# Block 0's feed-forward in two times 256 rows, gate and up with rows as stationary side, and query products at full rate: an adaLN transformer block on one Trainium2 core

## The chip, the cores and the metric

The kernel runs on one core of a Trainium2 chip. The metric is the device time of one execution in microseconds (us). The core's engines are TensorE (PE; its weight loads are shown as PEld), VectorE (DVE), ScalarE (ACT), GpSimd (POOL) and the queue of SyncE (SP), which issues the transfers here. Each engine works through its own instructions in order and waits on semaphores that the others raise.

## The reference

Inputs: 2048 rows of 512, all float32. Computed is one block with layer norms that a condition `c` scales and shifts:

```
mod = silu(c) @ w_mod                      # six rows of 512: sa, ca, ga, sb, cb, gb
h   = layernorm(x) * (1 + ca) + sa
q   = (h @ wq) in 32 heads of 16;  k = h @ wk;  v = h @ wv      # one k and v for all heads
p   = softmax(q @ k.T * 16**-0.5)
x   = x + ga * ((p @ v) @ wo)
h   = layernorm(x) * (1 + cb) + sb
x   = x + gb * ((sigmoid(h @ w_gate) * (h @ w_up)) @ w_down)    # 512 -> 1792 -> 512
```

## The kernel before

**Attention is the main line.** 2048 queries are cut into 8 query blocks of 256, the 32 heads into 4 groups of 8. A *unit* is one query block with one group, so there are 32 units (`units`), and each unit walks over the 16 blocks of 128 keys: 512 *steps*, each in two half-steps. In a step PE makes four score tiles `st` (128 keys by 512), whose exponentials ACT writes to `P`; four score tiles `sa` for a later unit (its row maxima are needed beforehand), which DVE reduces to `mx`; and, two steps late (`LAG`), the products of `P` and the values into `craw`. These are made in tiles of the array of 64 by 32, eight at a time (`columns`). At the end of a unit ACT copies `craw` to `cs`, and `place`, `recip` and `finish` normalise it with a round trip through DRAM; the last step of POOL gives `a`, the input of the output projection.

**Side work goes in between.** At the end of each half-step `piece` may append some products that don't belong to attention. A *term* is one product of 128 by 128 by 512 in float16 (every operand is split in a high and a low half and each product takes three passes); as side work a term is 8 matmuls of 64 by 32. Two groups of terms run together as a `Couple`, one in each half of the array's rows, and take both of the two PSUM banks that side work has. Side work is, in this order: the query products that the prologue left over (`q`, 5 couples of 24 terms), and for each block of 512 rows the output projection (`wo`, 2 couples of 24 terms), the norm on DVE and POOL, transposes (`tr`), gate and up (`gu`, 14 couples of 24 terms), and down (`dn`, 168 terms). Blocks 0, 1 and 2 are done inside the loop, and block 3 after it (the tail), with what is left of block 2 ahead of it.

**The planner.** `pick` chooses the next group, `plan` and `places` spread it over half-steps. The rates are terms for each half-step: `QRATE` 0.55 for query products up to step `FIRST`, `RATE` 2.2 for all else; `ERATE` applied only to early pieces, which `AHEAD` = 0, 0, 0, 0 switched off. Block `b` is handed over at query block 2b+1 (its first 256 rows: one `wo` couple and two `tr`) and at 2b+2 (everything else). A `wo` couple starts `SKIP` = 9 steps after its hand-over, a `tr` `GAP` = 2 steps after the norm is marked; if the next group isn't ready a spare one may go first, and if there is none, the half-step has no side work. `KEPT` = 2 groups at each block's end are kept as spares.

**Gate and up.** `gu_group(p, m)` holds the weights as the stationary side (128 of the 1792 columns) and moves `h2` (512 rows), so its result already stands with columns on partitions, as `dn` needs it. For each p ACT takes tanh of the gate's bank, DVE copies the up bank to `u`, and POOL makes (tanh + 1) * u and splits it in `gh` and `gl` (`gated`). `dn` comes in two parts (8 and 6 of the 14 pieces), each with its own read-out.

**Weights.** 46 jobs (`split_weight`) load the feed-forward's weights, scale and split them on POOL, and store gate's and up's to DRAM (`wD`), from where `ask` loads them back to the tiles `gw` (four of 512 KB, `GWB`), one for each p. 42 jobs are spread over the first `WSTEPS` = 110 steps. The last four overwrite the memory that holds the query weights (`wqh`, `wql` are parts of `wdh`, `wdl`), and come from step `WLAST` = 175 on.

## Time and profile before

| | us |
|---|---|
| median of 3 runs | 1707.36 (1706.1 to 1709.64) |
| profiled execution | 1703.12 |
| its span on the core | 1701.3 |
| prologue, to the first exponential of the loop | 105.6 |
| loop of 512 steps, to the end of the last `cs` copy | to 1559.9 |
| tail (block 2's rest and block 3) | 1559.9 to 1701.3 |

The engines overlap, so busy times don't add up; the question at any place is which of them the others wait for. The copy `cs` on ACT, once for each unit, is a good clock: from the end of one to the end of the next lie 16 steps. In what follows *unit n* in a time sense is the stretch that ends with the nth such copy, counted from 0; because of the lag of two steps it covers steps 16n+2 to 16n+17. A PE row of a group gives the time in which at least one of its matmuls ran, which overlaps with that of other groups.

### The profile page before, as it was taken

What the parts mean: (1) busy time and instruction counts of PE and PEld (TensorE: products, weight loads), DVE (VectorE), ACT (ScalarE), POOL (GpSimd) and SP (SyncE); (2) the same over time, 40 slices, a digit from 0 to 9 for tenths busy, and PEclk for the clock granted to TensorE, in tenths of its full rate; (3) what the DMA queues carried; (4) which work ended last, traced back from release to release, by engine and by line L of the source; (5) the groups of instructions that cost most, each with busy time, mean ns of one, the idle gap of its engine ahead of it and who ended that gap; (6) DMA issues with size and microseconds to landing.
All of it is one profiled execution on the core that took longest, in us unless ns stands there. A gap on an engine that the chain in (4) does not pass through costs nothing.

```text
span 1701.3 us, 88793 instructions
## 1 busy us (share of the span) xinstructions
PE 1657.1 (97%) x40226; PEld 997.2 (59%) x40226; DVE 1427.7 (84%) x2428; ACT 1287.3 (76%) x2335; POOL 610.2 (36%) x784
## 2 busy tenths in 40 slices
PE   6999999999999999999999999999999999999998
PEld 3335555555456666666656676666666676654443
DVE  7799999989999999999999999999999999912311
ACT  5558898878988888888888888888888888884100
POOL 4432554553242451232443232223442332132423
PEclk9989999999999999999999999999999999999999
DMA  7121333320121110111021110010121110011211
GB/s 243 54 62 49 107 104 99 110 77 21 29 62 50 58 54 14 40 28 28 28 77 52 50 42 13 28 37 25 38 77 41 52 53 16 23 47 52 87 50 38
DMA packets 86726, 94.12 MB, mean 55 GB/s; under 512 B 24916, under 2 KB 65868, under 8 KB 86348
## 3 DMA queue, kind: packets, MB, share of 16 engines
q1 hardware_dynamic: 86348, 88.44, 16.8%
q8 instruction: 315, 5.16, 1.3%
q14 instruction: 63, 0.52, 0.1%
HBM read 67.82 MB, written 16.24 MB: 49 GB/s over the span
## 4 chain that ended last, share of the span: by engine, by line
PE 81%; DVE 11%; ACT 3%; SPq 2%; DMA 2%; issue 1%; POOL 1%; POOLq 0%; ACTq 0%; DVEq 0%
PE craw L135 21%; PE pgu L135 15%; PE sa L135 13%; PE st L135 12%; DVE mx L135 8%; PE pd L135 7%; PE pgu L186 5%; PE pd L186 3%; PE po L135 2%; PE pq L135 2%; SPq L135 1%; ACT P L135 1%; DVE st L135 1%; DMA xall<-in_A_x_dram 1%; DMA lc<-lD 1%
## 5 line engine op out<-in xcount | busy, mean ns | idle before, releaser
L135 DVE TENSOR_REDUCE mx<-sa 128x1 f32<-128x512 f32 x2048 | 1288.6, 682 | 82.3 <-PE st L135 40.5
L135 ACT ACTIVATE P<-st 128x512 f32<-128x512 f32 x2048 | 1167.4, 597 | 226.2 <-PE st L135 168.6
L135 PE MATMUL craw<-P,V 64*32 64x512 f32 x8192 | 1094.7, 599 | 1.3 <-ACT cs L135 0.5
L135 PE MATMUL sa<-kp,qp 64*32 64x512 f16 (+1 forms) x7940 | 834.7, 379 | 13.1 <-DVE mx L135 12.4
L135 PE MATMUL st<-qp,kp 64*32 64x512 f16 x8192 | 837.6, 379 | 4.9 <-ACT P L135 4.2
L135 PEld LDWEIGHTS <-kp 64*32 64x32 f16 x8192 | 333.9, 91 | 215.9 <-issue 93.4
L135 PEld LDWEIGHTS <-qp 64*32 64x32 f16 (+1 forms) x7940 | 288.4, 92 | 149.6 <-issue 74.2
L135 PE MATMUL pgu<-h2h,gw 64*32 64x512 f16 x5248 | 285.4, 376 | 0.6
L135 PEld LDWEIGHTS <-gw 64*32 64x32 f16 x7872 | 181.7, 92 | 66.8 <-issue 25.1
L135 PEld LDWEIGHTS craw<-P,V 64*32 64x32 f32 x8192 | 184.0, 105 | 23.7 <-PE craw L135 4.1
L135 PE MATMUL pgu<-h2l,gw 64*32 64x512 f16 x2624 | 178.8, 376 | 1.2 <-issue 1.0
L135 PE MATMUL craw<-nought 64*32 64x1 f16 x1050 | 171.2, 163 | 0.0
L897 POOL TENSOR_SCALAR th<-th 128x512 f32<-128x512 f32 x41 | 25.4, 620 | 355.0 <-ACT th L135 298.2
L135 PEld LDWEIGHTS <-nought 64*32 64x32 f16 x1050 | 97.7, 93 | 71.9 <-issue 51.5
L556 POOL MEMSET qp<- 32x1024 f16 x60 | 56.7, 945 | 79.3 <-PE st L135 57.2
L320 POOL TENSOR_SCALAR wst<-wst 128x512 f32<-128x512 f32 x46 | 28.6, 621 | 155.5 <-DMA wst<-in_B_w_up_dram 103.2
L135 PE MATMUL pd<-wdl,gh 64*32 64x512 f16 x1152 | 79.2, 376 | 0.0
L135 PE MATMUL pd<-wdh,gh 64*32 64x512 f16 x1152 | 77.3, 376 | 0.1
L135 PE MATMUL pd<-wdh,gl 64*32 64x512 f16 x1152 | 76.6, 376 | 0.0
L186 PE MATMUL pgu<-h2h,gw 128*128 128x512 f16 x240 | 71.9, 379 | 1.5 <-DVE h2h L355 1.5
L891 ACT ACTIVATE th<-pgu 128x512 f32<-128x512 f32 x15 | 9.0, 597 | 82.1 <-PE pgu L186 82.1
L135 DVE COPY u<-pgu 128x512 f32<-128x512 f32 x41 | 28.0, 682 | 50.1 <-PE pgu L135 50.1
(160 smaller groups left out, 1436.9 us busy)
## 6 DMA issues: line engine op xcount, KB each, us to landing
gw<-wD SPq DMA_DIRECT2D x56, 512.0 KB
wD<-gw SPq DMA_DIRECT2D x14, 512.0 KB
wm<-in_w_mod_dram SPq DMA_DIRECT2D x6, 1024.0 KB
qp<-qD SPq DMA_DIRECT2D x192, 32.0 KB
qD<-q SPq DMA_DIRECT2D x16, 256.0 KB
xr<-in_A_x_dram SPq DMA_DIRECT2D x16, 256.0 KB
out_dram<-ot SPq DMA_DIRECT2D x16, 256.0 KB
raw<-cs SPq DMA_DIRECT2D x248, 16.0 KB
```

Of the source, the lines that this page charges most:

```text
L135: return (lambda *a, **k: keep(f_(*a, **k))) if pinned else f_
L186: pe.matmul(cut[0](self.bank) if cut else self.bank, l_, r_, start=(n == 0), stop=(n == self.n - 1))
L320: pool.tensor_scalar(w_, w_, SW, 0.0, op0=ALU.mult, op1=ALU.add)
L556: eng.memset(qp[j:j + 32], 0.0)
L891: act.activation(th, p_, AF.Tanh, scale=0.5 / (SH * SW))
L897: pool.tensor_scalar(th, th, 1.0, 1.0, op0=ALU.add, op1=ALU.mult)
```

## The change

- **Block 0's feed-forward is cut in two halves of 256 rows**, handed over at query blocks 1 and 2, each with everything from `wo` to `dn`. Before, only the first half's `wo` and `tr` were handed over at query block 1.
- **Gate and up of block 0** (`gu_rows`) hold 128 rows of `h2` as the stationary side and move weights: 512 moving columns are two pieces f of gate and of up. A couple is two blocks of 128 rows. Terms stay the same in number (24 for each of 7 couples in each half). The result stands with rows on partitions: ACT takes tanh of half of each bank, DVE copies the other half, POOL multiplies, and then `turned` transposes the product `g` with four transposes on PE (`pt3`), ACT copies the bank out, and POOL splits it.
- A turn of piece e (`gt`) follows couple e+1, and not before three steps after the mark of its own couple.
- **`dn` of block 0** runs over all 14 pieces at once, one couple of 84 terms for each half. Other blocks keep their two parts.
- **Rates**: `QRATE` 1.0; `ERATE` 1.65 for gate, up, turns and down of block 0 (`slow`); `RATE` 2.2 elsewhere.
- **Weights**: `WSTEPS` 95, `WLAST` 112. A `gw` tile holds two pieces (1 MB) and there are two of them; block 0 loads all weights twice, once for each half.

```diff
-QRATE = 0.55
-ERATE = 1.2
-AHEAD = 0, 0, 0, 0
+QRATE = 1.0
+ERATE = 1.65
-WSTEPS = 110
-WLAST = 175
+WSTEPS = 95
+WLAST = 112
-GWB = 4
+GWB = 2
 class Couple:
+        slow = False
 def gw_tile():
-        return P2.tile([P, 4, NDC, P], F16, tag="gw", name="gw", bufs=GWB)
+        return P2.tile([P, 2, 4, NDC, P], F16, tag="gw", name="gw", bufs=GWB)
 def ask(upto):
-                sp1.dma_start(gws[k], wD[fs[uses[k][0]]])
+                f = fs[uses[k]]
+                sp1.dma_start(gws[k], wD[f:f + 2].rearrange("f p a k n -> p f a k n"))
+        def gu_rows(t, e):
+            at = len(uses) // 2 * (t // 2) + e
+            def term(n, rs):
+                k, i = divmod(n, 3)
+                gw = gws[at]
+                h_, w_ = passes(*h2[k], 0, 1)[i]
+                return h_[rs, t * P:(t + 1) * P], gw[rs, :, w_:w_ + 3:2, k, :]
+            def end(p_, second):
+                gs_[t, e] = g_ = t32("g")
+                z = p_.rearrange("p (f m n) -> p f m n", f=2, m=2)
+                th, u_ = (g_[:, m * QU:(m + 1) * QU].rearrange("p (f n) -> p f n", f=2) for m in range(2))
+                act.activation(th, z[:, :, 0], AF.Tanh, scale=0.5 / (SH * SW))
+                dve.tensor_copy(u_, z[:, :, 1])
+                pool.tensor_scalar(th, th, 1.0, 1.0, op0=ALU.add, op1=ALU.mult)
+                pool.tensor_tensor(th, th, u_, op=ALU.mult)
+                marks[b, "g", t // 2, e] = now[0]
+            return Group("gu", 12, "pgr", term, end, (lambda: ask(at + GWB)) if t % 2 == 0 else None)
+        def turned(u, e):
+            pt = bank("pt3")
+            for f in range(2):
+                for t in range(2):
+                    pe.transpose(pt[:, (2 * f + t) * P:(2 * f + t + 1) * P], gs_[2 * u + t, e][:, f * P:(f + 1) * P], ident)
+            h32, hi, lo = t32("h32"), t16("gh"), t16("gl")
+            act.activation(h32, pt, AF.Identity)
+            pool.tensor_scalar(hi, h32, 1.0, 0.0, op0=ALU.mult, op1=ALU.add)
+            pool.tensor_tensor(lo, h32, hi, op=ALU.subtract)
...
+        if split:
+            halves = []
+            for u in range(2):
+                gs = [Couple(gu_rows(2 * u, e), gu_rows(2 * u + 1, e)) for e in range(NFC // 2)]
+                ts = [Turned(lambda n0, n1, u=u, e=e: turned(u, e), (b, "g", u, e)) for e in range(NFC // 2)]
+                seq = [gs[0]]
+                for e in range(1, NFC // 2):
+                    seq += [gs[e], ts[e - 1]]
+                seq += [ts[-1], Couple(down_group(2 * u, 0, NFC), down_group(2 * u + 1, 0, NFC))]
+                for z in seq:
+                    z.slow = True
+                halves.append([Couple(*wos[2 * u:2 * u + 2]), trs[u], trs[u + 2], *seq])
+            return halves
...
+            elif g.stage == "gt":
+                ok = s >= marks[g.mark] + GAP + 1
...
-            light = not q and g.stage == "gu" and s < 2 * NU * NKB + SKIP
+            light = g.slow
...
+        if o == 0 and b in (1, 2):
+            if b == 1:
+                blocks[0] = ffn_groups(0)
+            half = blocks[0].pop(0)
+            main.extend([*ready(0, half[:-1], i), (None, 1), *ready(0, half[-1:], i)])
```

**How the order moves, on DVE.** These are the DVE's rows from the first gate and up of block 0 on; `mx<-sa` are attention's reductions, four for each step, `u` and `g` the copies out of a side bank, `mh` the maxima for a later unit. Before:

```order
L135 TENSOR_REDUCE mx<-sa 128x1 x6
L135 COPY u<-pgu 128x512
L135 TENSOR_TENSOR mh<-m_13286,mh 32x64
L135 TENSOR_REDUCE mx<-sa 128x1 x22
L135 COPY u<-pgu 128x512
L135 TENSOR_REDUCE mx<-sa 128x1 x20
```

and in the change, which comes to this place at step 94 instead of 156:

```order
L134 TENSOR_REDUCE mx<-sa 128x1 x8
L134 COPY g<-pgr 128x256 x2
L134 TENSOR_REDUCE mx<-sa 128x1 x30
L134 COPY g<-pgr 128x256 x2
L134 TENSOR_REDUCE mx<-sa 128x1 x4
L134 RECIPROCAL rc<-lc 128x16
```

One copy of 512 has become two of 256, and between two couples lie some 30 reductions (seven and a half steps) where there were some 21 (five and a quarter).

**On POOL**, the products behind gate and up in block 0 (`th` or `g`) and the split in `gh` and `gl`. Before:

```order
L897 TENSOR_SCALAR th<-th 128x512
L898 TENSOR_TENSOR th<-th,u 128x512
L903 TENSOR_SCALAR gh<-th 128x512
L904 TENSOR_TENSOR gl<-th,gh 128x512
L556 MEMSET qp 32x1024 x2
```

and in the change, where `h_9801` is the turned product that ACT copied out:

```order
L893 TENSOR_SCALAR g<-g 128x256 x2
L894 TENSOR_TENSOR g<-g 128x256 x2
L557 MEMSET qp 32x1024 x2
L893 TENSOR_SCALAR g<-g 128x256 x2
L894 TENSOR_TENSOR g<-g 128x256 x2
L906 TENSOR_SCALAR gh<-h_9801 128x512
L907 TENSOR_TENSOR gl<-h_9801,gh 128x512
```

The split of a couple has moved behind the products of the next couple; the elements of each row together are the same.

**On PE, at the start of the tail** (`pr` is the last unit's normalisation). Before, a couple of block 2's gate and up was left for the tail:

```order
L135 MATMUL craw<-P_49032,V 32x512
L731 MATMUL pr_49136<-cs,picks 128x256 x4
L186 LDWEIGHTS gw
L186 MATMUL pgu<-h2h,gw 128x512
L186 LDWEIGHTS gw
L186 MATMUL pgu<-h2l,gw 128x512
```

and in the change the tail goes on with down:

```order
L134 MATMUL craw<-P_49308,V 32x512
L732 MATMUL pr_49436<-cs,picks 128x256 x4
L185 LDWEIGHTS gh
L185 MATMUL pd<-wdh,gh 128x512
L185 LDWEIGHTS gh
L185 MATMUL pd<-wdl,gh 128x512
```

Twenty-four matmuls of 128 by 512 have left the tail for the loop; the rest of the tail is the same, but that 36 instead of 65 `pd` matmuls now stand between the last `po` and the transposes of block 3's rows.

More of the change, by code (lines that the diff above doesn't have):

```diff
@@ L798, in ffn_groups @@
         HF = 8
-        ahead = 2 * AHEAD[b]
-        uses = [(p, 0) for p in range(ahead)]
-        uses += [(p, None) for p in range(NFC)]
+        split = b == 0
+        uses = [*range(0, NFC, 2)] * (2 if split else 1)
         asked = [0]
```

80 lines of the change are left out of this document (36 added, 44 removed).

## The prediction

> **What bounds the kernel now.** I read the page first: the totals, the engines over 40 slices, and the chain of waits.
>
> ```profile
> span 1701.3 us, 88793 instructions
> PE 1657.1 (97%) x40226; PEld 997.2 (59%) x40226; DVE 1427.7 (84%) x2428; ACT 1287.3 (76%) x2335; POOL 610.2 (36%) x784
> DVE  7799999989999999999999999999999999912311
> PE 81%; DVE 11%; ACT 3%; SPq 2%; DMA 2%; issue 1%; POOL 1%; POOLq 0%; ACTq 0%; DVEq 0%
> ```
>
> PE looks full from end to end, but that is an average over two regimes. The windows of the units show them; columns are stretch, its length, then busy time and instruction count of PE, PEld, DVE, ACT and POOL, then clock and transfers.
>
> ```profile
> 234.90:275.50 40.60, 40.39 (x930) 21.16 (x930) 39.73 (x69) 36.43 (x68) 19.86 (x26) 1.00 0.33 100
> 275.50:317.30 41.80, 40.80 (x929) 21.20 (x929) 39.91 (x69) 37.25 (x70) 21.48 (x27) 1.00 0.33 103
> 317.30:360.30 43.00, 41.33 (x994) 22.70 (x998) 40.29 (x69) 37.55 (x70) 20.72 (x27) 1.00 0.29 88
> 360.30:407.30 47.00, 43.97 (x1039) 24.06 (x1027) 42.23 (x75) 37.37 (x69) 27.48 (x38) 0.96 0.19 53
> 407.30:450.70 43.40, 42.58 (x897) 20.64 (x897) 41.62 (x73) 39.17 (x74) 9.80 (x13) 1.00 0.09 27
> 450.70:492.60 41.90, 41.62 (x990) 24.03 (x994) 40.90 (x71) 36.85 (x70) 8.45 (x11) 1.00 0.11 28
> 538.80:585.10 46.30, 46.13 (x1388) 31.20 (x1384) 43.09 (x72) 38.67 (x71) 17.11 (x20) 1.00 0.19 55
> 723.50:769.40 45.90, 45.89 (x1377) 31.18 (x1372) 43.22 (x72) 38.55 (x72) 14.73 (x17) 1.00 0.10 27
> 815.30:863.40 48.10, 46.77 (x1358) 31.49 (x1346) 45.87 (x78) 39.80 (x75) 19.91 (x25) 1.00 0.15 41
> ```
>
> These are units 3 to 8, 10, 14 and 16. The side work in three of them, by its tiles (PE busy, count): query products in unit 3, output projection in unit 8, gate and up in unit 10.
>
> ```profile
> 234.90:275.50 40.60, 7.74 (x128) 1.00 0.33 100
> 450.70:492.60 41.90, 8.98 (x192) 1.00 0.11 28
> 538.80:585.10 46.30, 25.85 (x580) 1.00 0.19 55
> ```
>
> A term is 8 matmuls, so these units carry 16, 24 and 72 terms. With 16 a unit takes 40.6 (unit 3) or 41.8 (unit 4), with 24 it takes 41.9: flat within its spread. From 24 to 72 it grows by 4.4 / 48 = 0.09 for each term. That isn't what a term costs PE, which is best seen in the tail, where PE makes the same products on the full array and waits for nobody:
>
> ```profile
> 1600.00:1640.00 40.00, 40.00 (x187) 18.09 (x186) 6.20 (x9) 3.58 (x6) 13.71 (x17) 1.00 0.28 93
> ...
> L186 PE MATMUL pgu<-h2h,gw 128*128 128x512 f16 x240 | 71.9, 379 | 1.5 <-DVE h2h L355 1.5
> ```
>
> 40 / 187 = 0.214 from one to the next (each lasts 0.38, but they overlap). So light units stand on something else, and DVE is it:
>
> ```profile
> 193.20:234.90 41.70, 39.60 (x68) 1.00 0.32 97
> L135 ACT ACTIVATE P<-st 128x512 f32<-128x512 f32 x2048 | 1167.4, 597 | 226.2 <-PE st L135 168.6
> ```
>
> The first row is DVE on the `mx` reductions alone in a light unit: 68 fill 39.6 of 41.7. ACT still waits 226 us over the run and has room. A light unit is thus a DVE unit of 41.5, a heavy one a PE unit of 46.1. They meet where 46.3 - 0.214 x (72.5 - n) = 41.5, at n = 50 terms. Units 0 to 8 carry 15 to 35; those from 10 on about 71. The unused room, some 30 terms in each light unit, is what the change can fill.
>
> **The change, part by part.**
>
> *Where block 0's work lands.* The planner's rate of 1.65 on 32 half-steps is 53 terms; turns take half-steps of their own, and the order of the built program shows 491 terms and 14 turns in the ten units 6 to 15, so 49 terms and 1.4 turns in each, right at the meeting point. Before, units 9 to 15 were heavy and took 815.3 - 492.6 = 322.7, 46.1 each. Blocks 1 and 2 are placed as before.
>
> *What a unit at 49 terms costs.* No stretch before has this load, so I bound it. Below: DVE's 41.5. Above: the straight line between 24 and 72 terms, 41.9 + 25 x 0.09 = 44.2. PE's own demand is 46.3 - 23.5 x 0.214 = 41.3. Near the meeting point both engines wait for each other through three `sa` and two `st` banks, so I put the terms at 42.8, between the ends.
>
> *What a turn costs.* Its nearest row is a transpose group of the norm's `tr`:
>
> ```profile
> 436.33 0.63 PE L135 MATMUL pt<-ident,t 128*128 128x128 f32 x4 [0.18 <-ACT q L135]
> 436.89 0.40 PE L135 MATMUL sa<-kp,qp 64*32 64x512 f16 x4
> 438.14 1.78 DVE L135 CAST h2h<-h 128x256 f16<-128x256 f32 x2 [1.06 <-ACT h L135]
> 440.57 0.40 PE L135 MATMUL sa<-kp,qp 64*32 64x512 f16 x4 [0.39 <-DVE mx L135]
> ```
>
> From the first transpose to the next attention product lie 0.56, change of array tiling included. The rest of what a `tr` costs comes from DVE, whose cast waits 1.06 for ACT with reductions queued behind it; a turn has no DVE instruction: ACT copies the bank out, POOL splits. Below: nothing (PE has slack in a DVE unit). Above: 0.56 and a bank held until ACT has emptied it, 0.6 for the copy, so 1.2. I take 0.6, 0.85 in each unit. With it a unit is 43.7; the bounds are 41.5 and 44.2 + 1.4 x 1.2 = 45.9.
>
> The Trainium skill's page TensorEngine Tiling (Array Packing), section Tiling Modes, says that a change of tiling mode, not only of the tile, drains the TensorE; that speaks against 14 turns in a loop of 64 by 32 tiles. If two drains came on top of the row, each by my estimate the 0.38 - 0.21 = 0.17 that a tail matmul outlasts its spacing, the sum below would end 4.6 higher, at about 1696; the row of 0.56 already holds both changes, so I add nothing.
>
> *Reading the banks.* Tanh and copy come in two pieces of 256 for each couple instead of one of 512. DVE's copy took 0.68, a 256-wide read of a bank on DVE in the tail 0.42:
>
> ```profile
> L135 DVE COPY u<-pgu 128x512 f32<-128x512 f32 x41 | 28.0, 682 | 50.1 <-PE pgu L135 50.1
> ...
> L737 DVE TENSOR_TENSOR raw<-pr,raw x1: 424/424/424, 1563.8 to 1563.8; 128x256 f32<-128x256 f32 x1
> ```
>
> Two halves are +0.17 for each of 14 couples, 2.4 on DVE in all; against it, `dn` in one part saves block 0 four read-outs of 0.7 on DVE or ACT. I take nothing. Tanh on ACT is covered by ACT's room. POOL's elements are the same and it is 36% busy.
>
> *The start of block 0.* Units 6 and 7 took 47.0 and 43.4 with few terms. The chain of waits in unit 6 shows why:
>
> ```profile
> 370.81 3.60 DMA wst<-in_B_w_down_dram
> 375.89 1.17 POOL wdl L322
> 377.05 1.24 POOL t L818
> 378.29 1.24 POOL xr L832
> 379.56 0.70 DVE st L135
> 381.10 0.40 PE sa L135 x4
> ```
>
> A weight's late transfer holds POOL, the norm's steps queue behind it, the norm's DVE row waits, reductions queue behind that, and PE waits for a bank. In the change `wo` and norm come at steps 73 to 86 while weights still run (to step 93), so nothing removes this; it moves to units 4 and 5. I keep 47.0 + 43.4 = 90.4 for these. If the norm misses the weights, 4 are gained; if it waits for two, 4 are lost.
>
> *The stretch of units 4 to 16* took 863.4 - 275.5 = 587.9. In the change: 90.4 + 10 x 43.7 + 1.5 (the second pair of `tr` with its DVE wait, which sat in units 7 to 9) + 47 (unit 16: rest of down, block 1's start; 48.1 before) = 575.9. That is -12.
>
> *Query products at 1.0* put 25 to 28 terms in units 0 to 3 instead of 15 to 17, still under 50; by unit 8 against the light units +0.3 each, with denser weight work on POOL: +1.
>
> *The tail.* 24 products of 0.214 leave it: -5.1. Less work then stands between the last `po` and block 3's second transposes. The norm's chain ran
>
> ```profile
> 1569.58 1.29 DVE L820 TENSOR_TENSOR t<-po,ga 128x512 f32<-128x512 f32 x2 [1.69 <-PE po L186]
> 1577.02 0.55 DVE L350 TENSOR_SCALAR t<-xr,mv,rs 128x512 f32<-128x512 f32 x1
> 1583.77 1.91 PE L854 MATMUL pt<-ident,t 128*128 128x128 f32 x16
> ```
>
> from 1569.6 to 1577.6, 8.0, under 65 products (13.9). Now 36 cover 7.7, and the first half's first transposes, 4 of the 16, 0.5 more: just enough; 0 to 1.5 lost. I take 0.
>
> *Weights read in 1 MB pieces*: 14 of them in block 0 over 120 steps. Transfers are at 0.10 to 0.19 of their share in the heavy units above, and each piece is asked for one couple (24 / 3.3 steps, 19 us) ahead. At the highest rate of the page's slices, 243 GB/s in the first, 1 MB takes 4.3, so it is hidden: 0. Without that cover each of 14 couples would wait 4.3, 60 in all.
>
> ```profile
> GB/s 243 54 62 49 107 104 99 110 77 21 29 62 50 58 54 14 40 28 28 28 77 52 50 42 13 28 37 25 38 77 41 52 53 16 23 47 52 87 50 38
> ```
>
> Sum: -12 + 1 - 5 = -16. The profiled execution had a span of 1701.3 and took 1703.12; it becomes 1685 and 1687. The median of the runs is 4.2 above that execution, so 1707.4 - 16 = **1691**.
>
> **The rivals.**
>
> *A sharp knee.* If DVE and PE overlap better than I think, units at 49 terms cost 42.2: 15 less, 1676. For it: unit 8 with 24 terms stands at the floor. Against: DVE's share of 95% there leaves little for waits.
>
> *No knee.* A unit at the meeting point costs 45.4, since each stall of one engine then reaches the other: +17, 1708, no change. For it: the line from 24 to 72 terms is nearly that with dear turns. Against: in heavy units DVE is at 93% and PE still at 99.7%, so PE loses next to nothing to it there.
>
> *Slower: the two side banks.* A turn takes one of two; the next couple needs both, a half-step later, and PE, being in order, stands before that couple's first product with attention queued behind it. ACT must first take the exponentials ahead (up to 1.2) and then copy 0.6. Likewise each couple's banks are now emptied by ACT and DVE in turns. At 1.6 for each of the 14 pairs of couple and turn above what I priced, 22 are lost: 1713. It ends above before from 19.4 / 14 = 1.4 for each pair on. For it: in-order PE, two banks. Against: a half-step of attention, 1.3, lies between turn and couple and covers most of the copy.
>
> That the change doesn't move the work is excluded by the order: gate and up begin at step 87.
>
> **How the numbers follow.** Forecast (units of 43 to 44.7) 0.45, sharp knee 0.22, no knee 0.13, side banks 0.20. Predicted is 1691; its own range is 1680 to 1702. The whole range, 1674 to 1714, takes in the sharp knee and the side banks. A difference under 0.2% (3.4 us) can't be told from none: faster 0.71 (forecast, sharp knee, a third of no knee), same 0.09, slower 0.20.
>
> **What would show it.** Right: units 6 to 15 at 43 to 44.7, DVE over 95% busy in them, a turn with the next attention product within 0.7, a tail 5 shorter, units 18 to 31 unchanged. Side banks: PE idle before `pgr` with ACT as releaser, 1 us or more, 14 times. No knee: the same units over 45 without any such wait. The forecast falls if the start of block 0 costs more than 95 instead of 90.4, since weights and norm then collide worse than before, or if units 0 to 3 pass 42.5.

## The result, and the profile after

The change made the kernel slower by 0.3%: 1712.17 us median (1707.8 to 1717.17, 20 runs) against 1706.6 (1701.99 to 1711.81, 20 runs) in the same comparison, a ratio of 1.0032 with a 95% interval of 1.0023 to 1.0042. The forecast was 1691, faster than before. The page of the changed kernel, in the rows shown before (totals, VectorE over 40 slices, chain of waits):

```profile
span 1708.7 us, 89331 instructions
PE 1656.0 (97%) x40446; PEld 1000.3 (59%) x40446; DVE 1430.7 (84%) x2440; ACT 1299.5 (76%) x2361; POOL 605.8 (35%) x808
DVE  7799999989999999999999999999999999931411
PE 84%; DVE 7%; ACT 3%; POOL 2%; DMA 1%; issue 1%; SPq 1%; POOLq 0%; ACTq 0%; DVEq 0%
```

On this level almost nothing has moved, except that PE's share of the chain went from 81 to 84% and VectorE's from 11 to 7%: VectorE bounds less of the run, as intended, and PE bounds more. What that is worth shows only by stage. The windows of units 3 to 8, 13, 15 and 16 (length, then busy time and count of PE, PEld, DVE, ACT, POOL, then clock and transfers):

```profile
240.80:283.20 42.40, 41.24 (x1026) 22.80 (x1026) 40.30 (x69) 37.84 (x71) 25.31 (x32) 1.00 0.38 120
283.20:326.60 43.40, 42.27 (x1046) 24.20 (x1050) 41.07 (x71) 37.91 (x72) 25.25 (x32) 1.00 0.37 117
326.60:379.10 52.50, 47.17 (x1106) 26.55 (x1098) 44.30 (x78) 39.71 (x75) 32.41 (x48) 0.93 0.32 103
379.10:424.60 45.50, 44.80 (x1200) 27.55 (x1194) 41.99 (x73) 39.16 (x75) 13.91 (x20) 1.00 0.21 66
424.60:469.70 45.10, 44.40 (x1198) 27.49 (x1194) 41.82 (x73) 39.33 (x75) 18.66 (x26) 1.00 0.24 78
...
696.50:741.80 45.30, 44.51 (x1199) 27.92 (x1195) 41.89 (x73) 39.55 (x75) 11.47 (x17) 1.00 0.13 38
786.70:830.00 43.30, 43.30 (x1214) 27.64 (x1210) 41.83 (x73) 37.37 (x69) 11.01 (x19) 1.00 0.06 15
830.00:877.50 47.50, 44.92 (x1213) 28.06 (x1210) 45.15 (x75) 40.00 (x75) 12.21 (x14) 1.00 0.12 36
```

The stages of both profiled executions, measured at the `cs` copies, beside the forecast:

| stage | before | forecast | after | after - forecast |
|---|---|---|---|---|
| to the loop's first exponential | 105.6 | 105.6 | 109.1 | +3.5 |
| units 0 to 3 | 169.9 | 170.9 | 174.1 | +3.2 |
| units 4 and 5 | 84.8 | 90.4 | 95.9 | +5.5 |
| units 6 to 15 | 455.1 | 438.5 | 450.9 | +12.4 |
| unit 16 | 48.1 | 47.0 | 47.5 | +0.5 |
| units 17 to 31 | 696.4 | 696.4 | 695.0 | -1.4 |
| tail | 141.4 | 136.3 | 136.2 | -0.1 |
| span | 1701.3 | 1685 | 1708.7 | +23.6 |

The first row isn't the change: the code ahead of the loop is the same in both. To compare single executions I therefore also use the span less the loop's start, 1595.7 before and 1599.6 after.

Three things are to be seen. The tail is 5.2 shorter, within a tenth of the forecast. Unit 5 costs 52.5, with the granted clock at 0.93. And the units that gate and up fill stand at 45.0 to 45.9 where 43.7 was forecast, while unit 15, with down alone, is at 43.3 with more terms, as these counts of `pgr` in unit 13 and `pd` in unit 15 show (8 matmuls a term: 48 and 51):

```profile
696.50:741.80 45.30, 19.77 (x384) 1.60 (x4) 1.31 (x4) 1.00 0.13 38
```

```profile
786.70:830.00 43.30, 20.78 (x408) 0.00 (x0) 0.00 (x0) 1.00 0.06 15
```

The rest of the text asks for unit 5, for these units, and for what each of the change's parts is worth.

### The profile page after: what moved, and what is told of

It reads as the page before. It is cut to its first block, busy times and chain, and to the rows that moved or that the text cites. A ratio compares the mean times of both kernels' runs of the same rounds, so it can differ in the third digit from the quotient of the medians.

```text
span 1708.7 us, 89331 instructions
## 1 busy us (share of the span) xinstructions
PE 1656.0 (97%) x40446; PEld 1000.3 (59%) x40446; DVE 1430.7 (84%) x2440; ACT 1299.5 (76%) x2361; POOL 605.8 (35%) x808
## 4 chain that ended last, share of the span: by engine, by line
PE 84%; DVE 7%; ACT 3%; POOL 2%; DMA 1%; issue 1%; SPq 1%; POOLq 0%; ACTq 0%; DVEq 0%
PE craw L134 23%; PE sa L134 14%; PE st L134 12%; PE pgu L134 10%; PE pd L134 7%; PE pgr L134 5%; PE pgu L185 4%; DVE mx L134 4%; PE pd L185 3%; PE pq L134 2%; PE po L134 2%; ACT P L134 1%; PE pt L134 1%; SPq L134 1%; DVE h2h L134 1%
## 5 line engine op out<-in xcount | busy, mean ns | idle before, releaser
L134 PEld LDWEIGHTS <-qp 64*32 64x32 f16 (+1 forms) x7940 | 279.2, 92 | 152.1 <-issue 74.8
L134 PE MATMUL pgu<-h2h,gw 64*32 64x512 f16 x3584 | 195.4, 376 | 0.7
L134 PEld LDWEIGHTS <-gw 64*32 64x32 f16 x5376 | 123.3, 92 | 44.7 <-issue 15.7
L134 PE MATMUL pgu<-h2l,gw 64*32 64x512 f16 x1792 | 122.6, 376 | 0.0
L920 POOL TENSOR_SCALAR th<-th 128x512 f32<-128x512 f32 x28 | 17.3, 617 | 251.8 <-ACT th L134 231.5
L134 PE MATMUL pgr<-gw,h2h 64*32 64x512 f16 x1792 | 104.3, 377 | 0.5 <-DVE g L134 0.5
L185 PE MATMUL pgu<-h2h,gw 128*128 128x512 f16 x224 | 67.0, 379 | 1.5 <-DVE h2h L356 1.5
```

What stands on the lines that cost most here:

```text
L134: return (lambda *a, **k: keep(f_(*a, **k))) if pinned else f_
L185: pe.matmul(cut[0](self.bank) if cut else self.bank, l_, r_, start=(n == 0), stop=(n == self.n - 1))
L920: pool.tensor_scalar(th, th, 1.0, 1.0, op0=ALU.add, op1=ALU.mult)
```

## Experiments

All kernels ran beside the kernel before on the same chip; the ratios are to it. Unless said otherwise an edit is made to the changed kernel.

### The start of block 0

The chain of waits of the changed kernel in unit 5 (start, length, what), and below it PE's rows of the transposes with the idle time before them:

```profile
333.55 3.09 DMA wst<-in_B_w_down_dram
...
336.71 0.63 POOL wst L321
...
338.33 1.11 POOL wdl L323
...
341.19 2.09 POOL t L351
...
343.33 0.90 PE pt L134 x3
```

```profile
343.33 0.90 PE L134 MATMUL pt<-ident,t 128*128 128x128 f32 x3 [5.01 <-POOL t L351]
346.05 1.11 PE L134 MATMUL pt<-ident,t 128*128 128x128 f32 x4
```

A weight of `w_down` is late, POOL splits it, the norm's last row `t` stands behind the split, and PE, in order, stands 5.01 before the block's second transposes with attention queued behind them. From 342.6, still in that wait, the granted clock is 0.50; the windows of that step and of the stretch of low clock:

```profile
337.50:348.24 10.74, 5.73 (x70) 2.65 (x65) 3.92 (x8) 4.30 (x9) 8.42 (x14) 0.74 0.56 211
```

```profile
342.60:349.40 6.80, 6.07 (x73) 2.98 (x81) 3.49 (x8) 3.81 (x8) 5.00 (x7) 0.50 0.13 37
```

The step took 10.74; the same step with its transposes takes 4.03 in the kernel with the hold below, 6.7 less. Of these 5.0 are the wait. The other 1.7, and 0.4 that the next step has more (3.12 for 2.71), are put down to the low clock: the 6.1 us of work in its stretch would cost up to 3.0 more at half clock, by my estimate. The page TensorE: Matmul & The Clock Gate of the Trainium skill, section HAM oscillation — how this bites in real kernels, says that an idle gap of PE of more than about 3.4 us throttles the clock; the gap here was 5.01, and the row agrees. But shorter gaps have been followed by a low clock too, as the last section shows.

**Weights held behind the norm (pause).**

```diff
+HOLD, RESUME = 33, 89
+                if HOLD <= wdone < nw - 4 and s < RESUME + 2 * (wdone - HOLD):
+                    break
```

> The change, but weight jobs 33 to 41 are held back from steps 77 to 93 to steps 89 to 105, past block 0's first norm. Theory A (at the start of block 0 a late weight transfer holds POOL, the norm's last step comes 5 us late, and PE stands before the transposes of step 86): that step falls from 10.7 us to 3 to 4, units 4 and 5 together from 95.9 to about 89, and the whole run is 6 to 8 us faster than the changed kernel, so level with before or 1 to 2 us faster. Theory B (the norm is late by its own length or by the transfers at a unit's end, whatever the weights do): step 86 stays over 8 us and the run within 2 us of the changed kernel.

Measured: 1706.95, ratio 1.0003 [0.9993, 1.0014]. Units 4 and 5 of this kernel:

```profile
282.50:326.80 44.30, 42.08 (x1046) 23.60 (x1050) 41.19 (x71) 38.00 (x71) 21.34 (x27) 1.00 0.30 97
326.80:372.20 45.40, 44.96 (x1106) 25.19 (x1105) 43.58 (x78) 39.32 (x74) 22.65 (x36) 1.00 0.35 113
```

Unit 5 lost 7.1 and the low clock, and units 4 and 5 together went from 95.9 to 89.7; the same 46 jobs, nine of them some 12 steps later, took away about the whole loss of the change by the ratios. Theory A holds by place. Its size, 6 to 8, wasn't reached: by the ratios the gain is 4.9. In the single profiled execution the span less the loop's start is only 1.8 below the change's, 1597.9; units 6 to 15 took 2.5 more, unit 16 1.9 and the tail 1.6. The last two each hold 3.4 us at clock 0.50, which the changed kernel's trace doesn't have there.

**Weights earlier (weights76)**: `WSTEPS` 95 becomes 76, so that the last of the 42 spread jobs is done before the norm.

> The change, with WSTEPS 76 instead of 95, so that the 42 spread weight jobs end at step 75, ahead of block 0's first norm, while the first 70 steps get a quarter more weight work on POOL. Theory A (late weights hold the norm): units 4 and 5 fall from 95.9 to 89 or less and, other than in the run with held-back weights, units 6 and 7 stay at 45.2, so 6 to 9 us faster than the changed kernel. Rival: POOL, then at about 70% in units 1 to 3, holds the query products' read-outs, and units 0 to 3 lose 3 us or more.

1707.41, ratio 1.0006 [0.9992, 1.0019]. Unit 5 fell to 45.1, and unit 4 rose from 43.4 to 47.9, so that the two took 93.0 where theory A gave 89 or less. The rival's loss in units 0 to 3 didn't come (173.3). The stall of step 86 goes here too (4.03), without a hold; why unit 4 rose is not shown; the denser weights are the likely reason.

**Transposes later (late_tr)**: block 0's `tr` may come six steps behind the norm instead of two.

```diff
-                ok = (b, g.u) in marks and s >= marks[b, g.u] + GAP
+                ok = (b, g.u) in marks and s >= marks[b, g.u] + (6 if b == 0 else GAP)
```

> The change, with the second transposes of block 0 allowed six steps behind the norm instead of two; nothing else. Theory A (the stall of step 86 is the norm's late arrival behind a late weight, so transposes that come later do not meet it): the step of 10.7 us goes, units 4 and 5 together 88 to 91 instead of 95.9, and the whole runs 5 to 7 below the change: 1704.5 to 1707.5, level with before. Rival N, the four steps are lost again because gate and up, the turns and down all move back by four steps and the rest spills into units 16 to 18 and the tail: units 16 and 17 3 us longer, time 1709 to 1712. Rival O, the stall follows the weights, not the transposes (POOL and the norm's rows are late whatever PE asks for first, reductions queue behind them): units 4 and 5 stay at 95, time 1711 to 1713.

1718.92, ratio 1.0091 [1.0068, 1.0115]: slower than any of the three expected. Its chain of waits shows that the stall only changed its place:

```profile
339.15 9.21 DMA wst<-in_B_w_down_dram
...
348.44 0.63 POOL wst L321
...
358.92 0.64 POOL h2l L357
...
359.60 0.63 PE pgr L134 x5
```

The transposes found the norm done, but the split of their result (`h2l`) stands on POOL behind weight splits and the last steps of a unit's end, and the first gate product waits for it. That is theory O in its mechanism. Units 4 and 5 took 93.9 (O: 95). The rest of the loss is in places that O didn't name: units 18 to 31 took 653.6 (649.6) and the tail 144.7 (136.2). Of the tail's 8.5, 24 products of gate and up that fell back into it make 5.1, and 6.8 us at clock 0.50 from 1580.7 on about 3.4. This profiled execution, 1727.85, was the slowest of the six, so its stages show more than the median's loss. The tail's `pgu` rows, of the changed kernel and of this one:

```profile
1572.50:1708.70 136.20, 72.84 (x336) 9.63 (x14) 8.36 (x14) 1.00 0.16 54
```

```profile
1581.30:1726.00 144.70, 79.48 (x360) 10.32 (x15) 8.96 (x15) 0.97 0.17 59
```

**The early constants alone (early_only)**: the kernel before with `QRATE` 1.0, `WSTEPS` 95 and `WLAST` 112, without the halves and the rows.

> The kernel before with only the change's early constants: QRATE 1.0, WSTEPS 95, WLAST 112. It takes block 0 as before. Theory L (query products at full rate and denser weights cost the light units something: from the loop's start to the end of unit 3 the changed kernel took 174.1 us, before 169.9): 170.5 or more of these remain here at about 174, and the run is 2 to 4 us slower than before. Theory M (those 4 us were chance, like the start of the loop at 105.6 to 110.0 in six traces): within 1.5 us of before.

1710.67, ratio 1.0031 [1.0017, 1.0044], the loss of the whole change. Units 5 and 6:

```profile
326.80:378.80 52.00, 43.54 (x817) 19.57 (x809) 42.68 (x76) 38.18 (x73) 30.07 (x44) 0.93 0.15 42
378.80:419.20 40.40, 39.83 (x801) 19.36 (x801) 39.63 (x69) 36.01 (x68) 6.10 (x8) 1.00 0.08 22
```

The same unit 5 of 52, and units 0 to 3 at 174.8. So the stall doesn't need the halves; it comes with the order that the full query rate makes. Before, a spare query couple lay between norm and transposes (they came at step 125); with the queries done by step 70 no spare is left, and the transposes come at step 86, right behind the norm.

**The query rate alone (q_only)**: the kernel before with `QRATE` 1.0 only.

> The kernel before with one constant of the change, query products at rate 1.0; weights stay spread over 110 steps, the last four from step 175. The three constants together cost 5.0 us (1710.67 against 1706.05). Theory L, the query rate alone does it: the denser query couples cost 4 to 5 in units 0 to 3, and the order that follows from them (output projection from step 73, second transposes right behind the norm) brings the stall near step 86; time 1710 to 1711.5, units 0 to 3 together 172 to 175 (before 169.9), unit 5 over 50. Rival M, the denser weight work does it: with weights at the old rate units 0 to 3 stay at 170 to 171 and no unit of 4 and 5 exceeds 47; time 1705 to 1707.5, no difference from before.

1708.45, ratio 1.0018 [1.0004, 1.0031]; units 0 to 3 173.5, unit 5 49.8. Theory L holds by place (M would have left these units at 170 and 47); the time lies between what L gave and what M gave, and the interval overlaps that of the three constants together, so the denser weights may cost 2 or nothing. Why units 0 to 3 cost 4 more is known in part: the steps in which a query couple ends take 3.36 to 3.76 from first exponential to first exponential, others there about 2.5, and four couples instead of two end before step 64, which makes about 2. Step 2 took 3.7 instead of 2.7 here and in the changed kernel, but not in the kernels with the hold or the earlier weights, which have the same query products.

**The same hold in the kernel before (before_pause)**: jobs 37 to 41 held from steps 98 to 108 to 110 to 118.

> The kernel before with its weight jobs 37 to 41 held from steps 98 to 108 to steps 110 to 118, behind its own output projection and norm; nothing else. Before shows steps of 4.57 and 5.70 us at 96 and 104. Theory X, these are the same meeting of weights and norm as at step 86 of the change: step 104 under 4, units 6 and 7 together 2 to 4 shorter (90.4 now), time 1702 to 1704, so that the hold is worth as much in before and what beat before was the hold. Theory Y, they are the cost of the output projection's end whatever the weights do: steps unchanged, time 1705 to 1707.

1704.08, ratio 0.9979 [0.9967, 0.9990]. Unit 6:

```profile
364.50:408.10 43.60, 42.85 (x1039) 23.48 (x1027) 41.92 (x74) 37.33 (x70) 20.71 (x29) 1.00 0.14 39
```

Unit 6 was 47.0 before, 3.4 more; step 104 fell from 5.70 to 3.00, and step 96 kept its 4.57. Theory X holds: before already had this meeting, at a smaller price, and the hold isn't a gain that belongs to the change. In before PE stood 2.22 there for a reduction of VectorE, and 3.4 us at clock 0.50 followed; with the hold this unit's clock stays at 1.00.

### What a unit of gate and up costs

**The turns left out (no_turns)**: without the four transposes and ScalarE's copy, POOL splitting the product as it stands.

```diff
-                    pe.transpose(pt[:, (2 * f + t) * P:(2 * f + t + 1) * P], gs_[2 * u + t, e][:, f * P:(f + 1) * P], ident)
-            act.activation(h32, pt, AF.Identity)
```

> The change without the 14 turns: no transposes on PE and no copy on ACT for gate and up of block 0; POOL splits the product as it stands, so block 0's down product multiplies untransposed values. Theory A (a turn costs the 0.4 to 0.5 us by which its step is longer, and the rest of the dear units comes from the terms): units 6, 7, 12 and 13 fall from 45.2 to about 44.2 and the run by 5 to 7. Theory C (a turn holds one of the two side banks and the next couple waits): these units fall to 43 or below, and the run by 17 or more. Theory D (the turns are hidden): less than 2.

1710.43, ratio 1.0024 [1.0014, 1.0035]: 1.7 below the change, with intervals that overlap. Units 6 and 7 fell to 44.4, as theory A gave, but the run by less than its 5 to 7; by time it is theory D. Units 6 to 15 together took 447.7, 3.2 less than in the change. This kernel leaves out the turns but keeps their half-steps empty.

**An own tile for the copied half (two_tiles)**: DVE's copy writes its own tile instead of half of the tile that ScalarE's tanh writes, so that it need not wait for the tanh.

> The change, but DVE's copy of the up half goes to a tile of its own (u) and not to the second half of the tile that ACT's tanh writes. In the changed kernel's trace the copy starts only when ACT's tanh is done (0.39 us), and the turn's transposes, which take the bank that both have read, stand 0.3 to 0.9 on PE behind the copy. Theory H (this row of waits, tanh, copy, bank, is what a turn and a couple's end cost): copy and tanh run side by side, the 3.09 us of a turn's step falls to about 2.75, units 6, 7, 12 and 13 from 45.2 to 44.5 or less, and the run by 4 to 6 us. Theory I (the bank is late by PE's own drain and the queue on ACT): the copy starts earlier and the run stays within 1.5 us.

1713.49, ratio 1.0044 [1.0029, 1.0060]. Theory I: no gain; that the copy starts behind the tanh costs nothing.

**The copy on ScalarE (act_copy).**

```diff
-                dve.tensor_copy(u_, z[:, :, 1])
+                act.activation(u_, z[:, :, 1], AF.Identity)
```

> The change, but ACT instead of DVE copies the up half. Theory J (DVE is the engine that the dear units wait for: its copies wait for the end of a couple with reductions queued behind): the couple-end steps fall from 2.94 to 2.7, units 6, 7, 12 and 13 by 0.8 to 1.2, the run by 6 to 9 us. Theory K (PE is the one; DVE has room at 49 terms): within 2 us, and slower if the bank is held longer, since ACT now reads it twice in turn.

1716.89, ratio 1.0064 [1.0047, 1.0081]. Taking 28 copies from VectorE made the units dearer, 45.9 to 46.0 instead of 45.1 to 45.5 (units 6 to 8), the slower branch of theory K. The steps say more: those with a turn fell from 3.09 to 2.82, and those in which a couple ends rose from 2.94 to 3.47, where ScalarE now reads the bank twice. So this run doesn't show that VectorE's copy is free; it shows that ScalarE is the dearer place for it.

**Neither copy nor tanh (no_copy, no_reads, no_copy_turns).** The first leaves out VectorE's copy (the product is tanh + 1 times itself), the second the tanh as well (constants instead), the third the copy and the turns.

> The change without VectorE's copy of the up half (28 copies of 0.42 us); the product takes the tanh half twice, so the output differs. A unit with 48 gate and up terms costs 45.2 (units 12 and 13), one with 51 down terms 43.3. Theory U, VectorE's read-out is what the forecast left out (in a unit that VectorE bounds every copy counts whole, 1.45 couples with 2 x 0.42 make 1.2): units 12 and 13 at 43.8 to 44.2, time 8 to 12 below the change, 1700 to 1704. Theory V, it is ScalarE's read-out and the bank held until it has come (giving the copies to ScalarE made units dearer by 0.4 to 0.7 though VectorE had less to do): units 12 and 13 at 44.8 to 45.3, time 1709 to 1713. Rival W, the products with rows as stationary side are dearer by themselves, whatever reads them: as V.

> The change without both read-outs of the gate and up banks (tanh and copy; the product is made of constants, the output differs); products, turns and POOL's work stay. Theory U: within 0.3 in a unit of the kernel without the copy alone. Theory V: units 12 and 13 at 43.5 to 44.2 here and near 45 there; time 1699 to 1704. Rival W, the products themselves: units 12 and 13 stay at 44.7 to 45.3 with neither read-out, time 1708 to 1713.

> The change without the copy of the up half and without the turns and their copy on ScalarE; the output differs. Without turns alone the units with 48 gate and up terms and no other work took 44.4 to 44.6 (13 and 14). Theory U: 43.0 to 43.4, the price of a down unit, so that copies and turns are all that gate and up cost above down; time 1698 to 1703. Theory V or W: 44.2 to 44.6, time 1707 to 1711.

1708.37, ratio 1.0010 [0.9997, 1.0023]; 1707.04, 1.0002 [0.9991, 1.0012]; 1710.68, 1.0021 [1.0008, 1.0034]. Units 12 and 13 of the kernel without read-outs:

```profile
646.80:691.10 44.30, 44.30 (x1199) 27.44 (x1195) 41.03 (x69) 38.22 (x70) 10.93 (x18) 1.00 0.19 62
691.10:736.20 45.10, 45.03 (x1199) 27.21 (x1195) 41.08 (x69) 38.16 (x71) 11.05 (x18) 1.00 0.13 38
```

With nothing to read out, PE is busy for all of 44.3. Without copy and turns the same two units took 45.1 and 44.7. That is neither U (43 to 44) nor V here and 45 there, and by these units it looks like W: read-outs are worth 0.2 to 0.8 in each of the two. Over units 6 to 15 the kernels without the copy, without read-outs, and without copy and turns took 446.9, 446.0 and 446.4, where the change took 450.9. The gains don't add up, and no run leaves out turns and both read-outs together. Where the rest sits is seen step by step. Windows of four steps of unit 13 in the changed kernel, carrying two terms in each half-step; one and two, the couple's last; a turn in the first half and two terms in the second; one and one:

```profile
708.19:710.90 2.71, 2.71 (x95) 1.89 (x87) 2.48 (x6) 2.28 (x5) 0.00 (x0) 1.00 0.07 17
710.90:713.84 2.94, 2.94 (x87) 1.64 (x71) 2.54 (x5) 2.71 (x7) 0.07 (x1) 1.00 0.05 8
713.84:716.93 3.09, 2.75 (x73) 1.86 (x77) 3.09 (x7) 2.86 (x7) 3.01 (x6) 1.00 0.66 187
716.93:719.42 2.49, 2.49 (x74) 1.36 (x60) 2.37 (x5) 2.26 (x4) 2.32 (x4) 1.00 0.62 248
```

The second of them without read-outs, and the third without turns and copy:

```profile
705.90:708.62 2.72, 2.72 (x87) 1.65 (x71) 2.59 (x5) 2.28 (x5) 0.00 (x0) 1.00 0.06 9
```

```profile
708.48:711.21 2.73, 2.28 (x70) 1.40 (x69) 2.26 (x5) 2.30 (x6) 0.94 (x2) 1.00 0.88 279
```

A couple's end costs 0.22, and it goes only when ScalarE's tanh goes (without the copy alone it stays at 2.94). A turn costs 0.36 in its step. Most of that is VectorE's copy: without the copy alone the turns' steps take 2.80 instead of 3.09, and PE's wait before the transposes, 4.2 in all in the changed kernel, is gone:

```profile
L134 PE MATMUL pt<-ident,g 128*128 128x128 f32 x56 | 9.2, 287 | 0.0
```

That is why the gains of leaving out copies and turns don't add. And the empty half-step costs as well: no terms and then two take 2.73, one and one 2.49; the turn with its empty half-step is thus 0.60, the size that the prediction gave a turn. Over all plain steps of units 6 to 16 the medians are 2.43 without terms, 2.50 for one and one, about 2.57 for two and one, 2.71 for one and two, and 2.71 to 2.75 for two and two. Gate and up and down don't differ in this: one and two take 2.72 and 2.71, two and one 2.55 and 2.56. In the kernel with the higher rate (below), where most steps have two and two, the medians are 2.72 over 57 steps of gate and up and 2.71 over 40 of down; one of each:

```profile
615.16:617.87 2.71, 2.71 (x95) 1.90 (x87) 2.48 (x5) 2.28 (x4) 0.00 (x0) 1.00 0.21 54
753.84:756.55 2.71, 2.71 (x98) 2.05 (x86) 2.71 (x6) 2.30 (x4) 2.11 (x2) 1.00 0.22 55
```

So rival W doesn't hold: with rows as the stationary side the products are no dearer than those of down in a step that is filled alike. The table of medians suggests that the second half-step sets a step's price. The next run tests this.

**The larger half first (big_first)**: of two unequal half-steps the larger goes first.

```diff
+                    if light and (at_ + k) % 2 == 0 and zs[k] < zs[k + 1]:
+                        zs[k], zs[k + 1] = zs[k + 1], zs[k]
```

> The change, but where a step of the slow groups has one term in its first half and two in its second, they are exchanged. Theory F (what counts is the half-step: steps with 1 and 2 terms take 2.71 us, as dear as 2 and 2, while 2 and 1 take 2.56): the 44 steps of that kind fall by 0.15 each, the run by 5 to 7. Theory G (only the mean load over several steps counts, and the two kinds of step differ just by where the trace cuts them): the other steps rise by as much, and the run stays within 2 us.

1710.81, ratio 1.0026 [1.0013, 1.0039]. The exchanged steps went from 2.71 to between 2.50 and 2.65, and the steps that had two and one before rose: all 42 of gate and up now have a median of 2.65, where 28 stood at 2.72 and 14 at 2.55. Units 6 to 15 fell by 1.5 and the run by 1.0 by the ratios, with intervals that overlap. This is theory G's size, not the 5 to 7 of theory F: that the second half-step sets the price is not borne out, and three terms cost about 2.65 in either order.

**A higher rate (rate22)**: `ERATE` 2.2.

> The change with block 0's rate at 2.2 instead of 1.65: the planned terms are 58, 56, 52, 64, 42, 58, 58, 52, 62, 30 in units 6 to 15 and 24 in unit 16, in place of 48, 48, 43, 58, 50, 56, 48, 48, 48, 52 and 60. Theory P (a straight line in the terms, 41.9 at 24 and 46.3 at 72): units 6 and 7 at 46 (45.0 and a turn's 1.0) where the change has 45.3, unit 15 at 42.5 (43.3), unit 16 at 45 (47.5); the sum stays and the time is within 2 of the change, 1709 to 1713. Rival Q (a knee that the change still sits below, so that terms above 50 are dear): units 6, 7, 11, 12 at 48 or more and light units no lower than 42; time 1714 to 1718. Rival R (a meeting point as forecast, each term above it at 0.214 and units below it at 41.5): units 6 and 7 at 44.5, unit 15 at 41.5; time 1704 to 1708.

1718.26, ratio 1.0072 [1.0054, 1.0090]. Units 11 (58 terms of gate and up, two turns, and one step of 4.21), 14 (62 terms of down) and 16 (24 of the output projection):

```profile
606.10:653.30 47.20, 45.59 (x1284) 30.17 (x1276) 42.00 (x73) 39.65 (x75) 11.54 (x17) 1.00 0.19 59
745.10:788.80 43.70, 43.70 (x1302) 29.55 (x1298) 42.14 (x73) 37.89 (x69) 11.05 (x19) 1.00 0.06 15
833.30:875.30 42.00, 41.66 (x990) 23.71 (x994) 40.75 (x71) 36.77 (x69) 8.49 (x12) 1.00 0.09 28
```

By time this looks like Q, but by the sum it is P: units 6 to 17 took 542.9 together, 543.8 in the change. P's single units don't all come out (unit 15 took 44.4 and not 42.5, unit 16 42.0 and not 45). The loss is in the tail, 141.7 instead of 136.2, where 360 `pgu` matmuls stand again instead of 336: 5.5 of the 6.1 by which the medians differ. Unit 14 is the clearest row on the price of terms: 62 of them, two in each half-step but one, cost 43.7, and 51 in unit 15 of the change 43.3.

### The rows as stationary side

**Columns again (columns)**: the halves stay, but weights are the stationary side as before, with 256 rows of `h2` moving, so that products and weight loads of block 0's gate and up double in number and turns fall away.

```diff
-                gs = [Couple(gu_rows(2 * u, e), gu_rows(2 * u + 1, e)) for e in range(NFC // 2)]
+                seq = [Couple(gu_half(u, e, 0), gu_half(u, e, 1)) for e in range(NFC // 2)]
```

> The change with halves, rates and weights as they are, but gate and up of block 0 with the weights as stationary side again: two pieces of 256 rows in one bank, so no turns; each term is 16 matmuls of 64 by 32 with 256 moving columns in place of 8 with 512. Theory A: like the kernel without turns, 5 to 8 us faster than the changed kernel, if the doubled weight loads hide behind the matmuls. Theory E (the stationary side was turned around because those loads don't hide): units 6, 7, 12 and 13 at 46 or more, the run 5 us or more slower than the changed kernel.

1744.62, ratio 1.0236 [1.0212, 1.0261]. Units 11 and 12:

```profile
621.30:671.30 50.00, 47.32 (x1631) 33.60 (x1627) 43.76 (x71) 39.24 (x71) 11.03 (x13) 0.97 0.18 56
671.30:720.70 49.40, 47.11 (x1623) 32.94 (x1619) 43.02 (x72) 39.38 (x71) 11.74 (x15) 1.00 0.21 58
```

PE's busy time in weight loads rose from 28 to 33 a unit and PE no longer fills its time (47.1 of 49.4). Theory E holds by its sign: halving the moving side costs 32 over the run, and of the two ways that were run the rows with their turns are the cheaper. Products and loads doubled together here, so the run doesn't tell which of them costs the 32.

### Both gains together (pause_big)

> The change with both edits that gained alone: weight jobs 33 to 41 held from steps 77 to 93 to steps 89 to 105, and of two unequal half-steps the larger first. Alone they ran at 1.0003 and 1.0026 of before, the change at 1.0032. Theory S, the two act in different places (start of block 0, regular half-steps) and add: 1705 to 1706.5, a ratio of 0.9994 to 1.0003, so no faster than before by more than can be told. Rival T, they overlap (the exchange gained in the stalled units 4 and 5): 1706.5 to 1708, no better than the pause alone.

1702.67, ratio 0.9985 [0.9973, 0.9997], the best time of a version with the halves. The kernel before with its own hold has 0.9979 [0.9967, 0.9990]; they cannot be told apart by these. The median is below what S gave (1705 to 1706.5), but the interval reaches S's ratios; T's times lie above all of it. In the profiled executions, from the loop's start to the end, the first takes 1596.9 and the second 1592.8. By the ratios both are below before and the change, and the hold is what they have in common.

## Why the prediction was wrong, point by point

**The start of block 0 (failed).** "I keep 47.0 + 43.4 = 90.4 for these" was the step; measured 95.9. The mechanism was named rightly, weights that hold POOL and the norm, and so was the alternative ("if it waits for two, 4 are lost", "falls if the start of block 0 costs more than 95 instead of 90.4"). What I missed is that the wait is paid by another engine at another place: in before VectorE's row was late, PE stood 2.22, and a spare couple lay ahead of the transposes; now the transposes stand first in PE's queue, PE stands 5.01, and 6.8 at half clock follow. The order has the transposes right behind the norm; I priced that as unchanged. With the hold the two units took 89.7, below the forecast.

**Query products (failed in size).** "+1" was +4.2. I took the price of terms from units with terms spread thinly and left out the ends of couples, which are about 2 of it; early_only and q_only have the same 3.6 to 4.9 without the halves.

**The unit at 49 terms (failed).** "With it a unit is 43.7" was the step; the ten units took 450.9 for 438.5, and those of gate and up 45.0 to 45.9. It is the largest miss, 12.4, and two terms of the sum make it. The first is the read-outs, at which "I take nothing" stands: without them the ten units took 446.0, 4.9 less. ScalarE's tanh makes a couple's end 0.22 longer, 3.1 for 14 of them; VectorE's copy holds the transposes of a turn, 0.29 in its step. The second is the price of the terms. By the step prices 14 turns are 8.4 (0.60 each), as the prediction had it; that size is luck, since the parts are the empty half-step with 0.24, the copy with 0.29 and the transposes with 0.07. With 3.1 for the ends of couples and the 1.5 for `tr`, 437.9 are left for the terms: 43.8 in a unit by this estimate, and not 42.8. That is the larger part, about 10 of the 12.4; the straight line's 44.2, which was the upper bound, is nearer. Down alone did come out (43.3 at 51 terms; 42.8 + 2 x 0.214 = 43.2), and plain steps of both kinds take the same. So the 1.0 in each unit is likely to lie in how gate and up are spread over the steps around turns and ends of couples; no run placed them as evenly as down, so the cause of that part stays open.

**The picture of a knee (failed).** Light units as VectorE's and heavy ones as PE's, meeting at 50 terms, isn't what the runs show. In units 6 and 7 of the change VectorE is at 92 to 93%, not over 95%, and PE at 98%. A step's price rises gradually with its terms, 2.43 without any, 2.50 with two, about 2.65 with three and 2.71 to 2.75 with four, with no sharp bend at three. "No knee" gave 1708 and 45.4 for the unit, the nearest of the rivals, but for the reason of stalls that reach each other, and before the products of gate and up PE shows hardly any: 0.5 in all before `pgr`, in the groups of the changed kernel from 360 to 870:

```profile
L134 PE MATMUL pgr<-gw,h2h 64*32 64x512 f16 x1712 | 99.5, 376 | 0.5 <-DVE g L134 0.5
...
L134 PE MATMUL pt<-ident,g 128*128 128x128 f32 x56 | 8.8, 281 | 4.2 <-POOL g L893 2.8 <-DVE g L134 1.3
```

**Side banks (the slower rival).** It gave a time, 1713, that fits by chance. Its sign, PE idle before `pgr` with ScalarE as releaser, is absent in the first row. A smaller wait of the same sort is in the second: PE stands 4.2 in all before the 14 turns, 0.3 each. The row names POOL's product first, but without VectorE's copy the wait is gone though POOL's product stays, so it is the copy.

**The drain that a change of tiling mode might add.** The prediction set the drain that the Trainium skill's page TensorEngine Tiling (Array Packing) states in its section Tiling Modes at 4.6 by an estimate, and added nothing. Without any turn the run fell by 1.7 and the ten units by 3.2, copy on ScalarE included, and in no_copy a turn's step is 0.07 longer than one without a turn, so no run here shows more than the row of 0.56 held.

**Right.** The tail (-5.2 for -5.1), units 17 to 31 as before, unit 16 (47.5 for 47.0), and the weights in pieces of 1 MB: no wait of PE for `gw` stands in the rows above. The closeness of the tail is in part luck: seven other kernels with the same products in it have 3.4 us of low clock at its start and take 137.8 to 137.9.

**The sum.** early_only alone costs 4.6 by its medians, and the change 5.6. The halves with rows bring nothing: units 6 to 15 took 450.9 where early_only took 444.5, and the tail gives 5.2 back. There seven full units of 321.5 / 7 = 45.9 stand beside three of 40.3 to 42.2; with the halves all ten stand at 45.1 on average. Spreading the same terms thinner gains little when a step with three costs 2.65 and one with four 2.71 to 2.75, and the turns, with 0.60 in each of 14 steps by the prices above, cost 8.4.

## What to carry to other kernels

When work is moved into a stretch that "has room", take the price of a filled step from the trace, rather than a line or a knee between averages over 16 steps, and count the ends of groups and the read-outs apart: taken at nothing, the read-outs were 4.9 here. A difference between steps is a price only when moving the work moves the time; the exchange of half-steps promised 5 to 7 and gave 1.0. And when a transfer's lateness is only kept, ask which instruction will stand first in the queue of the busiest engine behind it: late weights cost 3.4 in before, where PE stood 2.22 for VectorE, and 7.1 in the change, where it stood 5.01 itself. A change of order made for one purpose (here the query rate) should be run alone.

## What the runs showed of the hardware that was not expected

The loop's start lay at 105.6 to 111.7 in the profiled executions of kernels whose code ahead of it is the same, and goes with the granted clock there. The windows up to it, of before, of the change and of the kernel with the query rate alone:

```profile
0.00:105.60 105.60, 86.33 (x562) 37.06 (x567) 85.58 (x174) 47.69 (x77) 47.16 (x93) 0.95 0.43 141
```

```profile
0.00:109.10 109.10, 89.12 (x562) 37.94 (x567) 85.66 (x174) 47.80 (x78) 47.15 (x93) 0.91 0.42 137
```

```profile
0.00:111.70 111.70, 91.51 (x562) 38.19 (x567) 85.95 (x174) 47.83 (x78) 47.63 (x94) 0.88 0.40 134
```

At 0.95, 0.91 and 0.88 the same 562 matmul records fill 86.3, 89.1 and 91.5. So a single execution can be 3 to 6 us longer for a reason ahead of everything that a change touches, which is as much as this change cost; stages, or the span less the loop's start, are the safer comparison.

Inside the loop, too, stretches of 0.50 come and go between executions. At block 1's start in unit 16 PE waits 1.5 for a reduction, in the changed kernel (first row) and in the one with the hold (second); only in the second a low clock follows (third row). In before one followed the wait of 2.22 in unit 6 (fourth row).

```profile
858.54 0.40 PE L134 MATMUL sa<-kp,qp 64*32 64x512 f16 x4 [1.52 <-DVE mx L134]
854.38 0.40 PE L135 MATMUL sa<-kp,qp 64*32 64x512 f16 x4 [1.51 <-DVE mx L135]
856.60:860.00 3.40, 3.40 (x69) 2.08 (x64) 2.08 (x5) 1.39 (x3) 0.02 (x1) 0.50 0.04 7
381.40:384.80 3.40, 3.40 (x57) 1.61 (x49) 2.67 (x6) 1.71 (x3) 3.07 (x6) 0.50 0.00 0
```

So here a wait well under 3.4 can be followed by a low clock, and the same wait need not be; what decides it is open. A stage that differs by about 1.7 between two single executions may differ by this alone.
